# A SwiGLU feed-forward kernel without the matmuls that TensorE runs before its first transpose

## The chip, the core and the metric

The kernel runs on one core of a Trainium2 chip. The core has five engines that work side by side, each on its own stream of instructions: TensorE (PE, matmuls; its weight loads are listed apart as PEld), VectorE (DVE), ScalarE (ACT), GpSimd (POOL) and SyncE (SP, which here only issues transfers). They meet through semaphores. Transfers between the chip's memory (DRAM) and the core's on-chip buffers are issued by an engine's queue and carried by 16 DMA engines.

The metric is the device time of one execution in microseconds, the median over runs. A profiled execution also has a span, from its first instruction to its last; its own time is a little longer than its span.

## The reference

```python
S, D, F = 2048, 640, 1536          # x: (1, S, D), bf16
def reference(x, w_gate, w_up, w_down):
    g = silu(x @ w_gate)           # (S, D) @ (D, F)
    u = x @ w_up                   # (S, D) @ (D, F)
    return (g * u) @ w_down        # (S, F) @ (F, D)
```

All inputs are bf16. The output is (1, 2048, 640) in bf16.

## The kernel before

**Tiling.** P is 128. D is cut into KD = 5 pieces of 128, F into KF = 12 pieces of 128, and the 2048 rows of x into 4 blocks of S_BLK = 512. HALF is 256 rows. For each block, the kernel walks over the 12 pieces of F; for each it makes a gate tile `pg` and an up tile `pu` (128 columns of F by 512 rows of x, 5 matmuls each), ScalarE takes the Silu of `pg`, and VectorE multiplies it with `pu` into `aT`. Then the block is multiplied with w_down and written out. The last four rows of x are computed apart on VectorE, as dot products (`row_dots`), spread over the run.

**TensorE's operands.** A matmul takes a stationary operand (`lhsT`, loaded by a weight load) and a moving one (`rhs`); both need the summed dimension, here D, on the partitions. So x is wanted transposed, as `xT`. Most of `xT` is filled by transposing transfers (`turn_x`). The first 256 rows are not: they come as they are into `x_sb`, in two chunks of 128 rows, and TensorE transposes them itself against an identity matrix (`transpose_chunk`, L185: five transposes of 128x128 for each chunk), into a PSUM tile `pt` that ScalarE and VectorE copy into `xT` (L190).

**The head of the program.** SyncE and ScalarE first issue the transfers of the two x chunks (L86), then five transfers of the first four 128-column pieces of w_gate, one for each `kd` (L115, SyncE and ScalarE in turn). SyncE goes on with the transposing transfer of rows 256 to 511 (L105), the first pieces of w_up in two transfers (L83), and the rest of the weights. Meanwhile GpSimd makes the identity, VectorE fills a 128x128 tile `ones` with 1.0 (L109), and ScalarE runs a Silu over one column of it (L119, `silu_first`, whose result nobody reads), ahead of which it loads its function table.

TensorE's own stream is in the function `head`, which fixes its order by hand (`keep_order`):

1. `warm(N_WARM)`: 18 matmuls of `ones` with `ones`, 128x128 by 128 columns, into a PSUM tile `pw` that nobody reads (L176). They wait for VectorE's memset alone. These are called fillers below.
2. Ten transposes of x (L185). The first waits for the transfer of x_sb and for the identity.
3. Gate matmuls (L193) for the first EARLY = 4 pieces of F at once, one PSUM tile `pg` each: `kd` = 0 over rows 0 to 127 and then 128 to 255 (8 matmuls of 128 columns), `kd` = 1 to 4 over rows 0 to 255 (16 of 256 columns), then `kd` = 0 to 4 over rows 256 to 511 (20 of 256 columns).
4. The up matmuls for these four pieces, 5 of 512 columns each, into `pu`.

Behind `head` the loop over blocks goes on in the same manner, with matmuls of 512 columns. The tile `pw` shares a ring of four PSUM buffers (tag "gu") with `pg` and `pu`.

## Time and profile before

| | |
|---|---|
| median of 3 runs | 163.26 us |
| the runs | 162.93, 163.26, 163.68 us |
| the profiled execution's own time | 163.73 us |
| its span | 162.4 us |
| TensorE busy | 159.4 us, 98% of the span |
| VectorE busy | 111.1 us, 68% |
| ScalarE busy | 42.6 us, 26% |
| memory traffic | 6.88 MB read, 2.62 MB written |

In the page's lines on groups of instructions, a line has the source line, the engine, the operation, what is written and read, the count, then the busy time of the group and the mean length of one in ns, then the idle time of the engine just before them and what ended most of it. TensorE's matmuls overlap: one starts before the last one has come out at the other end, so the length of one (some 0.3 us for 128 columns) is more than the step from one start to the next, and it is the step that counts. A timeline merges neighbours of one kind into a line, with the start of the first, the time from there to the end of the last, and the count. The chain of waits goes back from the last instruction to whatever released each one; what stands on it sets the end.

The row PEclk on the page is the granted TensorE clock in 40 slices of the span, in tenths of full speed.

### The profile page before, as it was taken

To read this page: it belongs to the slowest core of one execution; us is meant where nothing else is said; L and a number is where in the kernel's file an instruction comes from. 1 tells how busy PE (TensorE), PEld (TensorE's weight loads), DVE (VectorE), ACT (ScalarE), POOL (GpSimd) and SP (SyncE) were. 2 spreads that over 40 slices of the span, in tenths; PEclk is the share of its full clock that TensorE was granted. 3 is DMA by queue.
4 is the path that set the end of the run, shared out by engine and by line. 5 is a ranking of instruction groups with operands and counts; after the bars stand their busy time and mean duration, and the time that the engine had idled before them with its cause. 6 is when DMAs were issued, how large, how long until landed. Compare 5 with 4: busy or idle time off the path is not lost.

```text
span 162.4 us, 2129 instructions
## 1 busy us (share of the span) xinstructions
PE 159.4 (98%) x796; PEld 78.0 (48%) x808; DVE 111.1 (68%) x250; ACT 42.6 (26%) x74; POOL 0.6 (0%) x6
## 2 busy tenths in 40 slices
PE   8999999999999999999999999999999999999995
PEld 8754444444444444444444444444444444445454
DVE  1024333499559999979919999979964999993101
ACT  5051222112232222221222322221214222222121
POOL 1000000000000000000000000000000000000000
PEclk9999999999999999999999999999999999999999
DMA  7999999995169997003110000000421000000212
GB/s 215 259 339 350 362 184 250 228 231 88 53 125 178 217 176 145 4 0 34 65 65 0 0 4 2 0 0 0 65 67 34 0 0 0 0 0 4 44 45 73
DMA packets 41961, 15.86 MB, mean 98 GB/s; under 512 B 33504, under 2 KB 41824, under 8 KB 41952
## 3 DMA queue, kind: packets, MB, share of 16 engines
q1 hardware_dynamic: 33440, 14.80, 38.0%
q10 hardware_dynamic: 8512, 0.94, 3.9%
q8 instruction: 6, 0.10, 0.3%
q14 instruction: 3, 0.02, 0.1%
HBM read 6.88 MB, written 2.62 MB: 59 GB/s over the span
## 4 chain that ended last, share of the span: by engine, by line
PE 97%; DMA 2%; issue 0%; DVE 0%
PE pg L193 32%; PE pu L193 32%; PE po_a L291 26%; PE po_t L261 6%; DMA x_sb<-in_x_dram 2%; PE pt L185 1%; DVE ot_b L302 0%
## 5 line engine op out<-in xcount | busy, mean ns | idle before, releaser
L193 PE MATMUL pg<-xT,wg_sb 128*128 128x512 bf16 (+3 forms) x258 | 60.1, 366 | 0.3
L193 PE MATMUL pu<-xT,wu_sb 128*128 128x512 bf16 (+1 forms) x239 | 59.0, 379 | 0.1
L215 DVE TENSOR_TENSOR aT<-sg,pu 128x512 bf16<-128x512 f32 (+1 forms) x48 | 32.8, 683 | 32.9 <-PE pu L193 32.9
L214 ACT ACTIVATE sg<-pg 128x512 f32<-128x512 f32 (+1 forms) x48 | 28.4, 596 | 71.5 <-PE pg L193 67.7
L291 PE MATMUL po_a<-wd_sb,aT 128*128 128x512 bf16 (+4 forms) x224 | 42.4, 348 | 0.2
L147 DVE SCALAR_TENSOR_TENSOR prod<-wgT,x_row 128x640 f32<-128x640 bf16 x48 | 39.4, 821 | 1.1
L147 DVE SCALAR_TENSOR_TENSOR prod<-wuT,x_row 128x640 f32<-128x640 bf16 x48 | 39.4, 822 | 1.0
L193 PEld LDWEIGHTS <-wg_sb 128*128 128x128 bf16 x264 | 26.3, 101 | 26.8 <-DMA wg_sb<-in_w_gate_dram 0.2
L193 PEld LDWEIGHTS <-wu_sb 128*128 128x128 bf16 x240 | 23.5, 98 | 28.0
L291 PEld LDWEIGHTS <-aT 128*128 128x128 bf16 x228 | 20.8, 98 | 21.7
L300 ACT CAST ot<-po_a 128x512 bf16<-128x512 f32 (+2 forms) x17 | 9.5, 560 | 31.8 <-PE po_a L291 20.6
L261 PE MATMUL po_t<-aT,wd_sb 128*128 128x512 bf16 (+1 forms) x47 | 10.3, 365 | 0.1
L261 PEld LDWEIGHTS <-wd_sb 128*128 128x128 bf16 x48 | 4.7, 98 | 5.1
L302 DVE CAST ot_b<-po_a 128x96 bf16<-128x96 f32 (+1 forms) x2 | 0.5, 242 | 9.7 <-PE po_a L291 9.6
L270 ACT CAST ot_t<-po_t 128x512 bf16<-128x512 f32 (+1 forms) x4 | 2.2, 560 | 11.6 <-PE po_t L261 11.6
L147 DVE DVE_READ_ACCUMULATOR prod<-wuT,x_row 128x1 f32 x48 | 3.9, 82 | 0.0
L147 DVE DVE_READ_ACCUMULATOR prod<-wgT,x_row 128x1 f32 x48 | 3.9, 82 | 0.0
L272 DVE STREAM_TRANSPOSE ot_q<-ot_t 128x512 bf16<-128x512 bf16 (+1 forms) x4 | 2.7, 678 | 1.7 <-ACT ot_t L270 1.7
L190 DVE COPY xT<-pt 128x384 bf16<-128x384 bf16 x2 | 0.7, 358 | 3.2 <-PE pt L185 3.2
L176 PE MATMUL pw<-ones 128*128 128x128 bf16 x18 | 2.1, 312 | 0.4 <-DVE ones L109 0.4
L176 PEld LDWEIGHTS <-ones 128*128 128x128 bf16 x18 | 1.8, 146 | 0.4 <-DVE ones L109 0.4
L119 ACT ACT_TABLE_LOAD x1 | 1.3, 1283 | 1.5 <-issue 1.5
(13 smaller groups left out, 4.7 us busy)
## 6 DMA issues: line engine op xcount, KB each, us to landing
wd_sb<-in_w_down_dram SPq DMA_DIRECT2D x1, 1920.0 KB, 14.2
out_dram<-ot SPq DMA_DIRECT2D x15, 128.0 KB, 1.7
wg_sb<-in_w_gate_dram SPq DMA_DIRECT2D x2, 640.0 KB, 8.3
wu_sb<-in_w_up_dram SPq DMA_DIRECT2D x2, 640.0 KB, 8.9
wu_sb<-in_w_up_dram SPq DMA_DIRECT2D x2, 320.0 KB, 5.4
x_row<-in_x_dram SPq DMA_DIRECT2D x1, 640.0 KB, 4.8
wg_sb<-in_w_gate_dram SPq DMA_DIRECT2D x3, 128.0 KB, 3.9
out_dram<-ot_q ACTq DMA_DIRECT2D x12, 32.0 KB, 2.0
```

The lines of the kernel that those rows point to most:

```text
L119: nc.scalar.activation(silu_first[:], ones[:, 0:1], ACT.Silu)
L147: nc.vector.scalar_tensor_tensor(out=prod[:], in0=wT[:, fc, :], scalar=1.0, in1=x_row[:, t, :], op0=ALU.mult, op1=ALU.mult, accum_out=acc[ ...
L176: nc.tensor.matmul(pw[:, 0:P], lhsT=ones[:], rhs=ones[:], start=True, stop=True)
L185: nc.tensor.transpose(out=pt[:, kd - k0, :], in_=x_sb[:, c, kd * P : (kd + 1) * P], identity=ident[:],)
L193: nc.tensor.matmul(ps[:, c0:c1], lhsT=w_sb[:, kd, fc * P : (fc + 1) * P], rhs=xT[:, kd, sb * S_BLK + c0 : sb * S_BLK + c1], start=(kd == 0 ...
L214: nc.scalar.activation(sg[:, 0:n_s], pg[:, 0:n_s], ACT.Silu)
L215: nc.vector.tensor_tensor(out=aT[:, fc, s0 : s0 + n_s], in0=sg[:, 0:n_s], in1=pu[:, 0:n_s], op=ALU.mult)
L261: nc.tensor.matmul(po_t[:], lhsT=wd_sb[:, kf, DA:D], rhs=aT[:, kf, sb * S_BLK : sb * S_BLK + n_t], start=(kf == 0), stop=(kf == KF - 1),)
L270: nc.scalar.copy(ot_t[:], po_t[:])
L272: nc.vector.transpose(out=ot_q[:], in_=ot_t[:])
L291: nc.tensor.matmul(po[:], lhsT=aT[:, kf, s0 : s0 + P], rhs=wd_sb[:, kf, c0:c1], start=(kf == 0), stop=(kf == KF - 1),)
L300: nc.scalar.copy(ot[:], po[:])
```

## The change

TensorE's stream begins with the first transpose: the 18 fillers, the function that issues them, their count and their PSUM tile are taken out. The tile `ones`, of which the one column that the first Silu reads is all that is still used, becomes 128x1. All else is as it was.

```diff
-    N_WARM = 18
...
-    ones = consts.tile([P, P], bf16)
+    ones = consts.tile([P, 1], bf16)
     silu_first = consts.tile([P, 1], f32)
     nc.vector.memset(ones[:], 1.0)
...
-    nc.scalar.activation(silu_first[:], ones[:, 0:1], ACT.Silu)
+    nc.scalar.activation(silu_first[:], ones[:], ACT.Silu)
...
-    pw = psum.tile([P, S_BLK], f32, tag="gu", name="pw", bufs=4)
-
-    def warm(n):
-        for _ in range(n):
-            nc.tensor.matmul(
-                pw[:, 0:P], lhsT=ones[:], rhs=ones[:], start=True, stop=True
-            )
-
...
-        warm(N_WARM)
         for c in range(HALF // P):
             transpose_chunk(c, split)
```

## The prediction

> **What bounds the kernel now.** I read the page first (engine shares, the chain that ended last, the granted clock), then the chain in order of time for the first 15 us, then TensorE's timeline in short stretches, and last the landings of the transfers that the head waits for. From the page of the profiled execution:

> ```profile
> span 162.4 us, 2129 instructions
> PE 159.4 (98%) x796; PEld 78.0 (48%) x808; DVE 111.1 (68%) x250; ACT 42.6 (26%) x74; POOL 0.6 (0%) x6
> PEclk9999999999999999999999999999999999999999
> PE 97%; DMA 2%; issue 0%; DVE 0%
> L176 PE MATMUL pw<-ones 128*128 128x128 bf16 x18 | 2.1, 312 | 0.4 <-DVE ones L109 0.4
> ```

> TensorE is the bound: 97% of the chain is its own work, and what comes ahead of it is one transfer. Whatever TensorE loses in the head arrives at the end. The fillers of L176 are 2.1 us of busy time, 18 instructions. The head of the chain, in order of time (start, length):

> ```profile
> 0.00 2.60 DMA x_sb<-in_x_dram
> 2.64 1.25 PE pt L185 x10
> 3.89 5.68 PE pg L193 x44
> 9.84 4.05 PE pu L193 x18
> ```

> The fillers are not on the chain. The first transpose waits for the first 128 rows of x, which land at 2.60; the fillers run inside that wait. So in themselves they cost nothing and their removal frees nothing. What they can do is act on TensorE's pace, which the timeline shows (start, length from the first start to the last end):

> ```profile
> 0.40 2.10 PE L176 MATMUL pw<-ones 128*128 128x128 bf16 x18 [0.40 <-DVE ones L109]
> ...
> 5.25 1.06 PE L193 MATMUL pg<-xT,wg_sb 128*128 128x256 bf16 x4
> ...
> 6.32 0.63 PE L193 MATMUL pg<-xT,wg_sb 128*128 128x256 bf16 x4
> ...
> 7.33 0.93 PE L193 MATMUL pg<-xT,wg_sb 128*128 128x256 bf16 x7
> ```

> To get the step from one start to the next, take the duration of the last instruction off and divide by the number of steps. Durations of the 256-column pg matmuls run from 0.27 (fast) to 0.42 (slow). At 5.25: (1.06 - 0.42)/3 = 0.213 us. At 7.33: (0.93 - 0.27)/6 = 0.110 us. The same instruction takes half the time; between them, at 6.32, the step is (0.63 - 0.27)/3 = 0.12, so the pace doubles at about 6.4 us. The fillers step (2.10 - 0.31)/17 = 0.105 us for 128 columns and the transposes (1.25 - 0.31)/9 = 0.104, as slow per column as the 0.213. So TensorE runs at half pace from its first instruction at 0.40 until 6.4, and at full pace after it. The granted-clock row says 9 from the first slice on, so it misses this start-up; I go by the steps.

> **The change part by part.** Set side by side, the instruction streams of the two programs are the same in order and waits except for this: TensorE loses 18 weight loads, 18 matmuls, their wait for the memset and one wait of the fourth pg tile for the fillers (same buffer, long met); VectorE's memset becomes 128x1. No transfer, queue or buffer changes place.

> The memset: 128x128 took 0.17 us (0.17 to 0.34). The nearest rows for 128x1 are GpSimd's memsets of constants, 0.10 us. VectorE's next work is at 3.39 and the Silu that reads the tile starts at 2.81, so both ends of that bound give 0.

> The fillers themselves: 0, since the transfer of x covers them (they end at 2.50, x lands at 2.60). If that cover were gone they would cost up to 2.1 us.

> The pace: this is the term that decides, and this trace shows only one rise, so it is bounded from both sides. Lower end: only the stretch from the first transpose counts. It is 6.4 - 2.64 = 3.76 us long, and without fillers it is the same: rise at 6.4, cost 0. Upper end for a rise that moves with TensorE's start: the time since the first matmul counts, 6.4 - 0.40 = 6.0, so the rise comes at 2.64 + 6.0 = 8.64, 2.24 us later. I take the value between them that follows from busy time: 2.10 of fillers + 3.76 = 5.86 us of work before the rise, so that without fillers it comes at 2.64 + 5.86 = 8.50, 2.10 us later. In 2.10 us at slow pace TensorE does 2.10/0.213 = 9.9 matmuls of 256 columns, which now take 9.9 x 0.110 = 1.08 us. Loss: 2.10 - 1.08 = 1.02 us (1.09 at the upper end).

> Does anything absorb it? Two transfers that the head waits for (issue to landing, queries for single issues at 1.86 and 3.51):

> ```profile
> xT<-in_x_dram SPq DMA_TRANSPOSE x1, 4.8
> ...
> wu_sb<-in_w_up_dram SPq DMA_DIRECT2D x1, 320.0 KB, 5.2
> ```

> The second half of x lands at 1.86 + 4.8 = 6.7 and is wanted at 4.63 + 16 steps, about 7.2; the first w_up columns land at 3.51 + 5.2 = 8.7 and are wanted at 9.4. Both are early already, so a later TensorE meets no wait that would shrink, and none of its inputs waits for it. Behind the head TensorE has no idle time to give. So the 1.02 us passes whole to the end. These landings also say what an earlier rise could bring: with full pace from 4.63, 16 x 0.110 = 1.76 ends at 6.39, the wait for x goes to 6.7, 20 x 0.110 = 2.2 gives 8.9 against 9.4. No run of before can be more than 0.5 us better than this one through the clock; the runs lie 0.8 below to 0.05 below its 163.73. In such an early run a rise 2.10 later, at 6.73, would cost (6.73 - 6.4) x 0.48 = 0.16 more than this execution, 0.66 more than itself. So the term lies between 0.66 and 1.09, if the fillers count.

> Sum: fillers 0, memset 0, pace +1.02. The span goes from 162.4 to 163.4 and the execution's own 163.73 to 164.75. The median of the runs, 163.26, stands 0.47 below that execution; the same addition gives 163.26 + 1.02 = **164.28 us**, 0.6% slower.

> [...]

> **The rivals.**

> 1. Not slower: the rise is set by the work from the first transpose on, wherever the fillers are. Place: the gap between the last filler's end (2.50) and the first transpose (2.64); point from which it decides: that gap breaks the busy stretch, or the fillers lie before the stretch that is judged. Price 0, time 163.26. For it: 3.76 us of nearly unbroken work (one wait of 0.15) is a stretch of its own, and with 2.1 us of fillers ahead the clock still had not risen by 6.0. Against it: the clock would then vary less or shift freely, and three runs of before were 0.05 to 0.8 us faster than the profiled one, more than the 0 that a fixed rise allows; a rise earlier than in the profile explains most of it (up to 0.5). [...]

> 2. Slower by more: the rise comes in whole stretches, and without fillers the first one judged is not full enough, so that a further 3.76 us go by at half pace: 3.76 x (1 - 0.110/0.213) = 1.82 us, 165.1. For it: the transposes and the 0.15 us wait for wg_sb at 4.63 then lie in the only stretch there is. Against it: the same work, from 2.64 on, was enough here by 6.4. [...]

> 3. Faster: the fillers stand in the way of the transposes. They end at 2.50, and x lands 0.10 later; from a landing before 2.50 each 0.105 us step of them delays the head. To gain 0.5% (0.8 us) x would have to land at 1.7 in the typical run. Against it: the wait for x_sb is on the chain here. A gain of 0.1 to 0.3, 163.0 to 163.2, is what it could give.

> That the edit does nothing is excluded by the instruction streams, apart from rival 1.

> **How the numbers follow.** Forecast 0.50, rival 1 0.28, rival 2 0.17, rival 3 0.05. The predicted time is the forecast's, 164.3, its own range 163.9 (0.66 more) to 164.6, with 0.2 for the scatter of a median. The range over the cases reaches down past rival 1 to 163.0 and up past rival 2 to 165.2. About what a measurement of this kernel can tell from no change is 0.5%, 0.82 us, so the line to slower is 164.08. Slower: rival 2 and nine tenths of the forecast, 0.17 + 0.46 = 0.63. Same: rival 1 and the forecast's low end, 0.28 + 0.04 = 0.32. Faster: 0.05.

> **What would show it.** Right: the first transpose again at 2.6; the step of the 256-column pg matmuls still 0.213 at 7 to 8 us and 0.110 only from about 8.5; the first pu matmul at about 10.4 in place of 9.4; everything behind it later by the same microsecond, transfers unchanged. Rival 1: the doubling at 6.4 again. Rival 2: doubling at about 10. Rival 3: first transpose earlier than 2.6. Wrong altogether: executions of the changed kernel whose rise jumps by more than 3 us from one to the next, or a span that grows without a later doubling.

## The result, and the profile after

| | before | changed |
|---|---|---|
| median of 16 runs | 163.55 us | 164.19 us |
| lowest, highest | 162.93, 163.82 us | 163.47, 164.90 us |
| profiled execution, own time | 163.73 us | 164.77 us |
| its span | 162.4 us | 163.4 us |

The ratio is 1.0045, with a 95% interval of 1.0027 to 1.0063: the changed kernel is slower by 0.74 us (0.44 to 1.03). The medians differ by 0.64 us. The two profiled executions differ by 1.0 us, more than the kernels do; why is part of what follows. The runs also scatter more without fillers: over 1.43 us, against 0.89 before.

The page of the profiled execution after:

```profile
span 163.4 us, 2105 instructions
PE 159.0 (97%) x790; PEld 76.7 (47%) x790; DVE 110.9 (68%) x250; ACT 42.5 (26%) x74; POOL 0.6 (0%) x6
PE 97%; DMA 2%; DVE 0%; issue 0%
```

TensorE is the bound as before. (This page has no PEclk row at all, the record holding no change of the clock.) The chain of the head, in order of time (start, length, what):

```profile
0.00 2.48 DMA x_sb<-in_x_dram
2.48 0.05 issue
2.53 1.25 PE pt L176 x10
3.77 6.65 PE pg L184 x44
10.42 4.32 PE pu L184 x20
```

The first transpose starts at 2.53 instead of 2.64, 0.11 us earlier, because x landed 0.12 earlier in this execution (2.48 and 2.60). The ten transposes take 1.25 us in both. The loss lies in the 44 gate matmuls: 6.65 us against 5.68, 0.97 us more. The timeline of TensorE shows why (start, length, count):

```profile
5.06 1.27 PE L184 MATMUL pg<-xT,wg_sb 128*128 128x256 bf16 x5
...
6.98 1.27 PE L184 MATMUL pg<-xT,wg_sb 128*128 128x256 bf16 x5
...
8.62 1.04 PE L184 MATMUL pg<-xT,wg_sb 128*128 128x256 bf16 x8
```

The steps are (1.27 - 0.42)/4 = 0.213 us at 5 and still at 7 us, where before they were 0.110, and (1.04 - 0.27)/7 = 0.110 from 8.6 on. One step between the two, of 0.140 us, begins at 8.26, which puts the doubling at 8.33 us instead of 6.4. The first up matmul starts at 10.26 instead of 9.40, and what follows runs as before, 0.86 us later. The spans differ by 0.97; the other 0.1 us arises in the last product (`po_a`), and the profiles don't show why.

### The profile page after: what moved, and what is told of

Read it like the earlier page. It is cut to its first block, busy times and chain, and to the rows that moved or that the text cites. A ratio compares the mean times of both kernels' runs of the same rounds, so it can differ in the third digit from the quotient of the medians.

```text
span 163.4 us, 2105 instructions
## 1 busy us (share of the span) xinstructions
PE 159.0 (97%) x790; PEld 76.7 (47%) x790; DVE 110.9 (68%) x250; ACT 42.5 (26%) x74; POOL 0.6 (0%) x6
## 4 chain that ended last, share of the span: by engine, by line
PE 97%; DMA 2%; DVE 0%; issue 0%
PE pg L184 33%; PE pu L184 32%; PE po_a L281 26%; PE po_t L251 6%; DMA x_sb<-in_x_dram 2%; PE pt L176 1%; DVE ot_b L292 0%
## 5 line engine op out<-in xcount | busy, mean ns | idle before, releaser
L184 PE MATMUL pg<-xT,wg_sb 128*128 128x512 bf16 (+3 forms) x264 | 61.4, 372 | 0.0
L281 PE MATMUL po_a<-wd_sb,aT 128*128 128x512 bf16 (+4 forms) x228 | 42.9, 348 | 0.0
L184 PEld LDWEIGHTS <-wg_sb 128*128 128x128 bf16 x264 | 26.8, 103 | 27.2
L251 PE MATMUL po_t<-aT,wd_sb 128*128 128x512 bf16 (+1 forms) x48 | 10.4, 366 | 0.0
L176 PE MATMUL pt<-ident,x_sb 128*128 128x128 bf16 x10 | 1.2, 308 | 2.5 <-DMA x_sb<-in_x_dram 2.5
L176 PEld LDWEIGHTS <-x_sb 128*128 128x128 bf16 x10 | 1.0, 138 | 2.5 <-DMA x_sb<-in_x_dram 2.5
```

What stands on the lines that cost most here:

```text
L176: nc.tensor.transpose(out=pt[:, kd - k0, :], in_=x_sb[:, c, kd * P : (kd + 1) * P], identity=ident[:],)
L184: nc.tensor.matmul(ps[:, c0:c1], lhsT=w_sb[:, kd, fc * P : (fc + 1) * P], rhs=xT[:, kd, sb * S_BLK + c0 : sb * S_BLK + c1], start=(kd == 0 ...
L251: nc.tensor.matmul(po_t[:], lhsT=wd_sb[:, kf, DA:D], rhs=aT[:, kf, sb * S_BLK : sb * S_BLK + n_t], start=(kf == 0), stop=(kf == KF - 1),)
L281: nc.tensor.matmul(po[:], lhsT=aT[:, kf, s0 : s0 + P], rhs=wd_sb[:, kf, c0:c1], start=(kf == 0), stop=(kf == KF - 1),)
```

## The experiments

Three theories. SUM, that of the forecast: the pace doubles after about 5.9 us of TensorE work. STRETCH: it doubles at the end of a stretch of some 3.4 us (3.413 in the bursts below) in which TensorE was busy nearly throughout, and the place of these stretches is not tied to the program's start. And, for the size of the effect, COVER: an early doubling is cut off by the transfers that the head waits for.

### The fillers alone

```diff
-    ones = consts.tile([P, 1], bf16)
+    ones = consts.tile([P, P], bf16)
```

This is the changed kernel with its tile of ones at the old size.

> The fillers are out, the tile of ones stays 128x128. All theories put the whole effect on the fillers and nothing on the memset: the time of the changed kernel, 164.0 to 164.4 us (ratio to the kernel before 1.003 to 1.006). If the smaller memset had a part, it would lie between the two kernels.

Median 164.09 us, ratio 1.0038 (1.0017 to 1.0059): as the changed kernel. The memset has no part that shows.

Its profile also tells against SUM. TensorE's instructions are those of the changed kernel, and the timeline begins as there:

```profile
2.69 1.25 PE L176 MATMUL pt<-ident,x_sb 128*128 128x128 bf16 x10 [2.69 <-DMA x_sb<-in_x_dram]
...
6.16 1.01 PE L184 MATMUL pg<-xT,wg_sb 128*128 128x256 bf16 x4
...
7.00 0.82 PE L184 MATMUL pg<-xT,wg_sb 128*128 128x256 bf16 x6
```

From 7.00 on the steps are (0.82 - 0.27)/5 = 0.110 us, and the clock record puts the doubling at 6.98. That is 4.3 us after the first transpose, some 0.1 of them waiting, where in the profile of the changed kernel it came after 8.33 - 2.53 = 5.8 us. The same work, then, does not bring the doubling at the same time. The span is 162.8 us instead of 163.4.

### Nine fillers early, nine late

```diff
-    N_WARM = 18
+    N_WARM = 9
```

> Nine fillers in place of 18, run from 0.40 to about 1.5 us, then TensorE idle for 1.1 us until x lands. Theory SUM (the pace doubles after about 5.9 us of work, wherever it lies): half of the effect is left, ratio 1.002 to 1.003, and the same as with nine late fillers. Theory STRETCH (the pace doubles at the end of a stretch of some 3.4 us, whose place is not tied to the kernel's start, when TensorE was busy in nearly all of it): the pause spoils each stretch that holds it, the nine fillers are worth nothing, ratio as without fillers, 1.0045.

The late ones have, besides, VectorE work ahead of the memset that they wait for:

```diff
...
+    nc.vector.memset(pad[:], 1.0)
+    nc.vector.scalar_tensor_tensor(out=prod[:, 0:512], in0=pad[:], ...)
     nc.vector.memset(ones[:], 1.0)
```

> The same nine fillers, but VectorE has 1.1 us of other work ahead of the memset of ones, so that they run from about 1.5 to 2.5 us, right ahead of the transposes. SUM: same time as with nine early ones, ratio 1.002 to 1.003. STRETCH: they lengthen the unbroken work by 1.1 us, ratio 1.001 to 1.003, and 0.2 to 0.5 us faster than nine early ones.

TensorE's timeline, first with nine early fillers:

```profile
0.40 1.14 PE L176 MATMUL pw<-ones 128*128 128x128 bf16 x9 [0.40 <-DVE ones L109]
2.66 0.61 PE L185 MATMUL pt<-ident,x_sb 128*128 128x128 bf16 x4 [1.12 <-DMA x_sb<-in_x_dram]
```

and with nine late ones:

```profile
1.68 1.14 PE L183 MATMUL pw<-ones 128*128 128x128 bf16 x9 [1.68 <-DVE ones L116]
2.69 0.61 PE L192 MATMUL pt<-ident,x_sb 128*128 128x128 bf16 x4
```

The same nine fillers, of the same 1.14 us, start 1.28 us apart; the transposes start within 0.03 us of each other. Early, they are worth nothing: 164.31 us, ratio 1.0053 (1.0034 to 1.0073). Late, 163.78 us, ratio 1.0016 (0.9999 to 1.0032). The intervals do not meet. It is not the amount of work that counts, so SUM falls; the idle 1.12 us between fillers and transposes takes the fillers' worth away, as STRETCH has it.

### Bursts

```diff
...
+        for k in range(4):
+            burst(90, 8 + k, False)
+            burst(90, 8 + k, True)
         for c in range(HALF // P):
             transpose_chunk(c, split)
```

A burst is 90 matmuls of 128 columns (or, where the last argument is True, 90 transposes), released by VectorE after a pause of 8 + k dummy operations.

> The changed kernel with eight bursts of 90 instructions of 128 columns put ahead of its transposes (matmuls and transposes in turn), with pauses of 8 to 11 us between them; some 130 us longer. Looked at: the time from the start of each burst to the doubling of its pace. SUM: the same in each burst, 3.8 to 6 us. STRETCH: it differs by up to 3.4 us from burst to burst, and the moments of doubling are whole multiples of one length, about 3.4 us, apart. If transposes count as work, the bursts of transposes show doublings as the bursts of matmuls do; if not, they stay at 0.107 us a step.

The starts of the first four bursts, in TensorE's timeline:

```profile
8.03 6.76 PE L188 MATMUL pb<-go 128*128 128x128 bf16 x90 [8.03 <-DVE go L182]
22.13 6.55 PE L186 MATMUL pb<-ident,go 128*128 128x128 bf16 x90 [7.34 <-DVE go L182]
36.88 7.66 PE L188 MATMUL pb<-go 128*128 128x128 bf16 x90 [8.20 <-DVE go L182]
52.74 6.61 PE L186 MATMUL pb<-ident,go 128*128 128x128 bf16 x90 [8.20 <-DVE go L182]
```

and the windows view, cut where the granted clock changes (from and to, length, PE busy and count, granted clock, DMA share, GB/s):

```profile
11.36:18.18 6.82, 3.44 (x61) 1.00 1.09 353
18.18:25.01 6.83, 2.88 (x28) 0.50 1.25 230
25.01:31.84 6.83, 3.67 (x65) 1.00 1.08 239
31.84:42.08 10.24, 5.20 (x49) 0.50 0.60 123
42.08:48.90 6.82, 2.46 (x43) 1.00 0.00 0
48.90:55.73 6.83, 2.99 (x29) 0.50 0.00 0
```

How full must a stretch be? Taking it that one busy share decides, two stretches bound it. In the second burst the stretch from 21.60 to 25.01 was busy from 22.13 on, 84%, and the clock rose. In the profile of the changed kernel the doubling at 8.33 puts the stretch before at 1.51 to 4.92; it was busy from 2.53 on, 70%, and the clock did not rise. By these two the mark lies between.

### The head at full pace

To see what an early doubling can bring, the transfers are held back by 9 us of VectorE work, and fillers run through that time:

```diff
-    N_WARM = 18
+    N_WARM = 140
...
+    for _ in range(9):
+        nc.vector.scalar_tensor_tensor(out=prod[:], in0=pad[:], ...)
+    for c in range(HALF // P):
+        nc.vector.tensor_copy(out=x_sb[:, c, 0:P], in_=prod[:, 0:P])
     load_x(nc.sync, 0, 1)
```

> The kernel before, with its first transfers held back by some 9 us of VectorE work (and 140 fillers in place of 18 to fill that time), so that TensorE is at full pace before x lands, whatever the phase. Looked at: the time from the first transpose to the first up matmul, 6.77 us in the kernel before and 7.73 in the changed one. Theory COVER (an early doubling is cut off by the transfers of the second half of x and of w_up, so the fillers can bring at most about 0.5 us below the profile of before): about 6.2 to 6.4 us, with TensorE waiting for xT or w_gate. Rival NO COVER (the head follows TensorE's pace alone): 10 + 8 steps of 0.056 and 36 of 0.11, about 5.0 us, without waits.

TensorE's timeline, 170.7 us of span:

```profile
11.72 0.85 PE L196 MATMUL pt<-ident,x_sb 128*128 128x128 bf16 x10 [0.96 <-DMA x_sb<-in_x_dram]
12.46 2.68 PE L204 MATMUL pg<-xT,wg_sb 128*128 128x128 bf16 x24
15.49 2.35 PE L204 MATMUL pg<-xT,wg_sb 128*128 128x256 bf16 x20 [0.35 <-DMA xT<-in_x_dram]
17.67 0.59 PE L204 MATMUL pu<-xT,wu_sb 128*128 128x512 bf16 x2
```

From the first transpose to the first up matmul: 17.67 - 11.72 = 5.95 us, a little under the 6.2 to 6.4 expected and far from 5.0. The third line shows the limit: after 24 gate matmuls TensorE stands idle for 0.35 us until the second half of x (xT) has landed. So in this execution no doubling, however early, could take the head below about 5.9 us, 0.8 us better than in the profile of before (6.77). Here that transfer landed 3.85 us after x, in the profile of before 4.08, which would leave about 0.6. In the profile of the changed kernel it landed 4.19 us after x, and with 21 fillers (below) only at 7.02 us, where it was 6.68 before and 6.67 in the changed kernel. So the limit varies and can lie closer still.

### The gap closed, and the kernel before once more

```diff
-    N_WARM = 18
+    N_WARM = 21
```

> 21 fillers in place of 18: they reach up to the landing of x and close the gap of 0.33 us between the last filler and the first transpose. STRETCH (a stretch counts when it is about 70 to 84% busy): the gap is only a tenth of a stretch, so the doubling comes earlier in few phases and mostly where the transfers cut it off: ratio 0.998 to 1.001. Theory GAP (the gap breaks the busy stretch and costs the fillers most of their worth): faster by 0.3 us or more, ratio 0.998 or less.

Median 163.21 us, ratio 0.9981 (0.9968 to 0.9995): somewhat faster than both kernels. The value lies on the border between the two expectations, so it doesn't tell them apart; a profile of the last pair of kernels below does.

> The kernel before once more, for a second profile. STRETCH: the moment of doubling is somewhere in 3.2 to 7.1 us, not again at 6.4; with a doubling before about 5.4 the first up matmul starts at about 8.9 and TensorE waits for the second half of x. SUM: doubling at 6.4 again.

The doubling came at 5.8 us, and the span was 162.1 us, 0.3 less than the first profile of this kernel, for a doubling 0.56 earlier. By the moment alone it would not be decisive against SUM, since the transposes too began earlier. Counted as work, without the waits, it came after 5.1 us, against 5.5 in the first profile by the same count. The transposes began on the fillers' heels, which the chain of the head shows:

```profile
0.39 2.10 PE pw L176 x18
2.49 1.07 PE pt L185 x10
```

In this execution x landed at 2.14, before the last filler was issued, and the first transpose began at 2.29, some 0.1 us later than it would have without fillers. So the delay of rival 3 is real in some executions. Here it cost nothing, since behind the transposes TensorE stood waiting for w_gate, which landed at 3.49 (weight loads, with the idle time ahead of them):

```profile
3.53 0.77 PEld L193 LDWEIGHTS <-wg_sb 128*128 128x128 bf16 x8 [0.24 <-DMA wg_sb<-in_w_gate_dram]
```

The wait for the second half of x that was expected for doublings before 5.4 was not put to the test at 5.8. With 21 fillers, where it doubled at 5.74 and xT landed late, at 7.02, it can be seen in the chain:

```profile
3.88 3.16 PE pg L193 x24
7.03 0.03 issue
7.06 2.34 PE pg L193 x20
```

The chain stops after 24 gate matmuls, the place at which the second half of x is first read.

### The same fillers where no transfer cuts in

A pair of kernels in which the first transpose waits for VectorE until 11.3 us, when the transfers of the head have landed, one with the 18 fillers, from 2.4 us ahead of it on, and one without. `pause(n)` stands for n dummy operations on VectorE:

```diff
...
+    pause(9)
     nc.vector.memset(ones[:], 1.0)
+    pause(2)
+    nc.vector.memset(pad[:], 1.0)
+    nc.vector.tensor_copy(out=gate_ident[:], in_=ident[:])
...
-                    identity=ident[:],
+                    identity=gate_ident[:],
```

> No fillers, and the first transpose held back to about 11 us by VectorE work, so that the transfers that cut an early doubling off have landed long before TensorE asks for them; some 8 to 8.5 us longer than the kernel before. Read against its twin with fillers. No wait for a transfer in the head; doubling 2.9 to 6.3 us after the first transpose.

> The same with the 18 fillers, started 2.2 us ahead of the first transpose as in the kernel before. COVER (the shift of the doubling is the full 2.1 us, and it measured less than 1.02 us because early doublings are cut off by the transfers): here, where nothing cuts them off, the fillers bring 0.95 to 1.1 us against the twin without them. Rival SHIFT (the doubling itself is moved by less than 2.1 us): 0.6 to 0.75 us, as between the two kernels.

Means of six runs: 172.71 us without fillers, 171.49 with; ratios to the kernel before 1.0563 (1.0537 to 1.0588) and 1.0491 (1.0467 to 1.0515). Six runs each leave too wide an interval, so both ran again:

> The held-back head without fillers once more, since six runs of each twin left 1.2 us with about 0.5 either way. Both theories: about 172.7 us.

> The held-back head with the 18 fillers once more. With both sets together, COVER: 0.95 to 1.1 us less than the twin without fillers; SHIFT: 0.6 to 0.75 us.

Ratios 1.0567 (1.0532 to 1.0602) and 1.0509 (1.0477 to 1.0541). With all twelve runs each, the means are 172.77 and 171.66: the fillers bring 1.11 us (0.72 to 1.49), 1.22 in the first round and 0.99 in the second. COVER's 0.95 to 1.1 fits; SHIFT's 0.6 to 0.75 reaches the interval's lower end only. It speaks for COVER without excluding the other. So does the scatter: here it is much the same with fillers (1.24 us) and without (1.29), while of the two kernels the one with fillers scatters less (0.89 against 1.43), as it should if its early doublings are cut off. (In its other rounds the kernel before scattered over 0.67 to 0.91 us, but in one, with a single run far out, over 1.96.)

The profile of the first round's kernel with fillers shows more:

```profile
8.87 2.10 PE L192 MATMUL pw<-ones 128*128 128x128 bf16 x18 [8.87 <-DVE ones L122]
11.30 0.80 PE L201 MATMUL pt<-gate_ident,x_sb 128*128 128x128 bf16 x6 [0.32 <-DVE gate_ident L125]
...
12.17 0.33 PE L209 MATMUL pg<-xT,wg_sb 128*128 128x128 bf16 x3
```

At 12.17 the steps are (0.33 - 0.22)/2 = 0.055 us, and the single starts put the doubling at 12.0, only 0.7 us after the first transpose. The stretch before it, from 8.6 on, holds a gap: the last filler's step was over at 10.77, the first transpose began at 11.30. If a gap of 0.53 us broke a busy stretch, the doubling could not have come before some 2.4 us of transposes and gate matmuls (70% of a stretch). So GAP falls, in this execution, and what counts is how much of a stretch is busy. Counted by steps, 76% of this one was, which narrows the mark to 70 to 76%. If the end of the last filler counts too (the view's idle time is only 0.32), it is 82%, and the mark stays nearly where it was. Just behind, TensorE waited 0.23 us for ScalarE's copy of `xT`: no transfer cut this early doubling short, but the copy did in part.

## Why the prediction came out as it did

**Direction and time.** Forecast 164.28 us, measured 164.19; but the median of before, too, came out higher over 16 runs, 163.55 instead of 163.26, and the effect is 0.74 us where 1.02 was forecast. That the two times agree to 0.1 us is thus partly luck. The forecast effect lies just inside the interval (0.44 to 1.03).

**The parts at nothing.** Fillers and memset cost nothing, as said: the first transpose waits for x in both profiles, and the kernel without fillers but with the large memset takes the changed kernel's time. The cover for the fillers, x landing at 2.60 in the one profile, is thinner than assumed, as the second profile of before shows (2.14).

**The pace, +1.02.** The mechanism was right: the fillers act through TensorE's pace, and a later doubling goes to the end at about half its delay. By the steps, a delay costs 1 - 0.110/0.213 = 0.48 us for each us; between the spans of the two profiles it is (163.37 - 162.41)/(8.33 - 6.37) = 0.49. Two things in the term were wrong.

First, the value came from busy time (5.86 us of work before the rise), and there is no such sum: nine fillers count or don't, according to where they lie, and one and the same stream doubled after 4.3 and after 5.8 us. What fits these profiles and the bursts is that the doubling comes with the first stretch of the 3.41 us grid that is full enough (somewhere in 70 to 84% busy by the two stretches above). An estimate from these numbers: with a first transpose at 2.6, that mark and every phase of the grid equally likely, the doubling without fillers falls evenly between about 5.0 to 5.5 and 3.41 us later. With fillers from 0.40 and 0.35 us of gap behind them, it falls from 3.1 to 3.6 on: earlier by 1.85 on average, not far from the 2.10 that the wrong reason gave. The profiles of the two kernels happened to lie 1.96 us apart, so their difference of 1.0 us agrees with the forecast by chance of two phases.

Second, the 0.5 us limit that the prediction worked out for early doublings (0.6 to 0.8 by the head at full pace) was used for its own range (0.66 to 1.09; its numbers make the upper end 1.08) and not for its value. It should hold for many of the runs of before: doublings before about 4.7 to 5.4 us (a head of 5.9 to 6.3 us at the least) bring nothing more, and by the estimate above that is three to seven tenths of the phases. (Where the second half of x lands late, even a doubling at 5.74 ran into the wait, as the profile with 21 fillers shows.) Cut off there, the average doubling that counts is 5.2 to 5.8 with fillers and 6.7 to 7.2 without; 1.1 to 1.7 us at 0.49 make 0.55 to 0.8, and 0.64 to 0.74 were measured. Where no transfer cuts in, the measured worth was 1.11. But without any cut the estimate is 1.85 at 0.49, or 0.9, and that lies inside both measured intervals (0.44 to 1.03 and 0.72 to 1.49). So the waits for xT, the pair and the scatter support the cut as the reason for the smaller size; the times do not prove it.

**Rival 1 (nothing) and rival 2 (a whole stretch more)** are not other kernels but other phases of this one. The fastest run without fillers, 163.47, is below the median with them; the slowest, 164.90, is near rival 2's 165.1. By the grid a given phase yields either the same doubling with and without fillers or one a whole stretch later, which is what the two rivals say; the forecast stands between them because it is near the mean of their prices, 0.9. This follows from the grid and was not measured, as no two runs are known to share a phase. The prediction took a rise that jumps by more than 3 us between executions for a sign of being wholly wrong. The runs of the changed kernel scatter over 1.43 us, at 0.49 some 2.9 us of doubling; the twelve with the large memset over 1.67 us, some 3.4, a whole stretch. So such jumps may well occur; on the grid they are no more than phase.

**Rival 3 (fillers in the way)** delayed the first transpose by about 0.1 us in one profile, where a wait for w_gate swallowed it. Nothing of it shows in the times.

## What to carry to other kernels

Idle TensorE time ahead of the first data was worth filling with matmuls here (0.74 us for 18 of them), where they ran nearly up to the moment when the real work started: what counted is how much of a stretch of 3.41 us was busy, not the number of fillers. Counted from step to step, a gap of 0.53 us was borne in one profile; one of 1.3 took the worth of nine fillers away. What it brought is about half of the time by which the pace rose earlier (0.48 to 0.49 us for each us), and in the late start with 140 fillers only down to the next transfer that the head waits for (0.35 us idle until xT), so look up those landings before the gain is put at its full size. Where the start-up depends on a phase, two profiles may differ by more than the kernels, as here by 1.0 us against 0.74; read the phase in each (the moment at which the step between matmuls halves, 6.37 and 5.8 us in two profiles of one kernel) before their difference is explained.

## What was not expected of the hardware

The expectation left open whether transposes count like matmuls for the clock. Here they do: in the bursts of transposes the clock rose 2.88 and 2.99 us after the start of the first two, and 90 of them took 6.55 to 7.62 us in the four bursts, the matmuls 6.76 to 7.66. The trace lists both as MATMUL.

In these traces the record of the granted clock starts with the first change (at 6.37 us before). The 1.00 in the views ahead of it (0 to 6.4 us before, 0 to 11.36 us with the bursts) is not a measurement: the steps of 0.107 us for 128 columns show half pace there, and 0.056 after the rise (61 matmuls of the bursts in 3.44 us).
